# Two transformer layers with segmented memory attention on one core: the memory update in column tiles, one pool of eight PSUM banks, and a newly made order of the work

## The chip, the cores and the metric

The kernel runs on 1 core of one Trainium2 chip. The metric is device microseconds of that core. Before the change three runs took 550.18, 549.96 and 549.16 us, a median of 549.96 us.

## The reference

The input is one sequence of 2048 tokens of width 640 in bfloat16. Two equal layers follow each other, with the same weights in both:

```python
x = x + A(layernorm(x))     # attention with a memory
x = x + B(layernorm(x))     # relu(x @ w1) @ w2, inner width 1728

# A: 32 heads of 20, four segments of 512 tokens, per head and segment s:
p     = softmax(qs @ ks.T * scale + causal mask)
a_dot = p @ vs
a_mem = (phi(qs) @ M) / (phi(qs) @ z + 1e-6)   # phi(t) = t + 1 if t > 0 else exp(t)
o     = g * a_mem + (1 - g) * a_dot            # g = sigmoid(beta), one number per head
M     = M + phi(ks).T @ vs                     # memory update, used by the next segment
z     = z + sum(phi(ks))
# A returns o @ wo
```

## The kernel before

**Who sets the order.** The program is not written in the order in which it runs. Every part of the work is a generator (a stream) that hands out operations with an engine, a guessed duration and the events that they wait for. A planner, class `Sched`, runs on the host while the kernel is built. It always takes the operation that can start first by its own guesses, with priorities, a few margins and a table `SHIFT` of hand-set shifts per stream and segment, and appends it to its engine's queue. On the chip each engine then works through a fixed list. The planner's guesses are no times of the chip and are not used here.

**The work on TensorE (PE).** A segment needs K and Q (the weights stay in the array, 512 tokens stream), V, the scores, the weighted sum of V ("apply"), the memory read and the memory update, the output projection and the two products of the feed-forward part. Nearly all products run through the helper `group`, so that they carry the lines L715 (one matmul on the whole 128x128 array) or L718 (the same product as four matmuls, each on a column tile of 32 columns, which run side by side). Other lines: L1236 scores, L1330 apply, L1369 apply for two special head groups, L1116 memory read, L1173 memory update (`mem_write`), L1510 the last 64 inner columns of the feed-forward part.

**Three tile shapes.** Scores contract over 20 features, so four heads run side by side in four row tiles ("rows"). Apply and L1510 run in column tiles ("cols"). Everything else can run on the whole array ("full") or as four column tiles; `_mode` chooses: it stays in the shape that the array has, and when it comes from rows it goes to cols if a product that needs cols is near.

**Scores.** For two head groups of four heads there are five rounds of two halves, done two halves at a time: 160 visits of PE in all, each with four or eight matmuls into two pairs of PSUM banks. After each visit ScalarE (ACT) runs two exponentials over 1024 columns each (L1298), GpSimd (POOL) cuts the causal triangle (L1310), and PE applies the result to V. One visit thus feeds two exponentials, and a pair of banks comes free when its exponential is done.

**PSUM.** Eight banks of 512 float columns. Banks 0 to 3 are two pairs that belong to the scores alone (`X`, `Y`). Banks 4 to 7 (`MISC`) take every other product, each until VectorE (DVE) or ACT has copied it out; early on, banks 4 and 5 are lent to the scores as a third pair (`Z`). The memory read uses one bank of MISC at a time in all segments but one.

**The memory update.** In 6 of the 8 passes over a segment (not the last segment of a layer) `mem_write` multiplies phi(k), transposed by DMA, with V: four blocks of 128 tokens times five chunks of 128 features, as a part of three chunks and a part of two, with widths of 147 and 168. That is 20 steps per pass, 120 in all. Whole-array steps compute all head pairs of a chunk, of which only the blocks of the same head are used. In column tiles only the first block of 128 tokens does so; the other three blocks let each of the four tiles compute just the two or three heads that it holds, widths 42 or 63. Which form a step takes is left to `_mode`.

**Copies out of PSUM.** `evac` lets the planner choose ACT or DVE for each copy: L916/L917 for Q and K, L971 for V, L1340 for the applied scores, L1534/L1535 for the feed-forward part. DVE adds the output projection to x in L1452 and the feed-forward part in L1556.

Of the kernel before, what the change touches and what calls it, by code (L numbers as in the profile page):

```python
# [13 lines left out]
NSEG = 4  # L14
# [96 lines left out]

class Op:
# [4 lines left out]
    def __init__(self, alts, waits, dma=None, acq=None, urgent=False, take=(), mode="full", lag=0.0, port=False):  # L117
        self.lag = lag
        self.port = port
        self.alts = alts  # L120
        self.mode = mode
        self.cols = None
        self.cols_ns = None
        self.acq = acq
        self.waits = [t for t in waits if t is not None]
        self.dma = dma
        self.urgent = urgent
        self.take = take


class Slot:
    def __init__(self, ap=None, name=""):
# [3 lines left out]
        self.tks = []  # L136

    def release(self, *tks):
        assert not self.free, self.name
        self.tks = [t for t in tks if t is not None]  # L140
        self.free = True

# [18 lines left out]
class Spawn:  # L161
# [7 lines left out]
LONE_NS = 300.0  # L169
SWITCH_NS = 96.0  # L170
COLS_LAG = 1500.0
SOFT = 400
SOFT_DMA = 1000
SOFT_FROM = ("sc",6,4,1)
# [3 lines left out]
SHIFT = {  # L178
# [9 lines left out]
}  # L188
# [3 lines left out]
class Sched:  # L192


    def __init__(self, prog):
# [8 lines left out]
        self.soon = 0.0  # L204
        self.landed = set()
        self.done = 0
        self.seen = 0
        self.live = []

    def add(self, prio, gen):  # L210
        self.streams.append([prio, gen, None, None, False])
        self.rank[id(gen)] = 0

    def at(self, tk):
        return self.t[(id(tk[0]), tk[1])]
# [5 lines left out]
    def _fill(self, st):  # L221
        while st[2] is None and not st[4]:
            try:
                y = next(st[1]) if st[3] is None else st[1].send(st[3][0])
            except StopIteration:
                st[4] = True
                return
            st[3] = None
            st[2] = y

    def _settle(self, st):

        while True:
            self._fill(st)
            if st[4]:
                return False
            y = st[2]
            if isinstance(y, (Op, Either)):
                return True
            if isinstance(y, Spawn):  # L240
# [3 lines left out]
            elif isinstance(y, Need):  # L244
                if y.key not in self.events:
                    return False
                st[2], st[3] = None, (self.events[y.key],)
            else:
                s = self._pick(y.slots)
                if s is None:  # L250
                    return False
                s.free = False
                st[2], st[3] = None, (s,)

    def _pick(self, slots):
        return min((s for s in slots if s.free), default=None,
                   key=lambda s: max([self.at(t) for t in s.tks], default=0.0))
# [8 lines left out]
    def _alts(self, op):  # L266
        res = []
        waits = op.waits
        if op.acq is not None:
            s = self._pick(op.acq)  # L270
            if s is None:
                return res
            waits = waits + s.tks
        for k, (e, hold, fns, tail) in enumerate(op.alts):
            m = PE_MARGIN if e == "pe" else 0.0
            if op.cols_ns is not None and self._mode(op) == "cols":
                hold = op.cols_ns
            if e == "pe" and self._mode(op) != self.mode:
                hold = hold + SWITCH_NS
            start = max([self.at(t) + SEM_NS + m for t in waits], default=0.0)  # L280
            start = max(self.free[e], start)
            if e == "dve" and op.port and self.free["pool"] > start:
                hold = max(hold, self.free["pool"] - start + PORT_NS)
            res.append((start + hold, start, k, e))
        return res

    def _landing(self, op):
        start = max([self.free["pe"]] + [self.at(t) + SEM_NS + PE_MARGIN for t in op.waits])
        soft = SOFT_DMA if SOFT_FROM in self.events else 0.0
        return max([0.0] + [self.at(t) + SEM_NS + PE_MARGIN + soft - start for t in op.waits  # L290
                           if (id(t[0]), t[1]) in self.landed])

    def _late(self, op):
        late = 0.0
        if op.alts[0][0] == "pe" and SOFT_FROM in self.events:
            waits = op.waits
            if op.acq is not None:
# [1382 lines left out]
```

## Time and profile before

| | |
|---|---|
| median of 3 runs | 549.96 us (549.16 to 550.18) |
| span of the profiled execution, first to last instruction | 548.1 us |
| the profiled execution's own time | the page gives its span alone |
| PE busy | 541.5 us (99%), 9714 matmuls |
| DVE busy | 422.0 us (77%) |
| ACT busy | 411.0 us (75%), 320 exponentials of them 309.1 us |
| POOL busy | 192.6 us (35%) |
| granted TensorE clock | 1.000 |

A matmul is recorded from its start to the end of its way through the array, and the next one starts before that. So busy time says when PE had something under way, and pace must be read from starts: from the start of one group to the start of the next. Times within the span are counted from its start.

### The profile page before, as it was taken

What the parts mean: (1) busy time and instruction counts of PE and PEld (TensorE: products, weight loads), DVE (VectorE), ACT (ScalarE), POOL (GpSimd) and SP (SyncE); (2) the same over time, 40 slices, a digit from 0 to 9 for tenths busy, and PEclk for the clock granted to TensorE, in tenths of its full rate; (3) what the DMA queues carried; (4) which work ended last, traced back from release to release, by engine and by line L of the source; (5) the groups of instructions that cost most, each with busy time, mean ns of one, the idle gap of its engine ahead of it and who ended that gap; (6) DMA issues with size and microseconds to landing.
All of it is one profiled execution on the core that took longest, in us unless ns stands there. A gap on an engine that the chain in (4) does not pass through costs nothing.

```text
span 548.1 us, 21884 instructions
## 1 busy us (share of the span) xinstructions
PE 541.5 (99%) x9714; PEld 313.9 (57%) x9715; DVE 422.0 (77%) x1057; ACT 411.0 (75%) x530; POOL 192.6 (35%) x307
## 2 busy tenths in 40 slices
PE   8999999999999999999999999999999999999998
PEld 6643465466544556545555554654566646757756
DVE  5999898899998668678998985787997689717202
ACT  5999968889888777887888889779897798041140
POOL 6345532433354334433344443333234333100000
PEclk9999999999999999999999999999999999999999
DMA  9899996545567254252656934525776241531301
GB/s 302 228 188 223 222 193 135 159 97 80 70 151 163 37 88 101 60 115 76 99 173 125 140 58 122 135 20 87 112 178 93 72 68 23 106 63 16 88 2 51
DMA packets 131910, 61.96 MB, mean 113 GB/s; under 512 B 112136, under 2 KB 121864, under 8 KB 131816
## 3 DMA queue, kind: packets, MB, share of 16 engines
q1 hardware_dynamic: 131384, 60.20, 52.4%
q8 instruction: 76, 1.25, 1.0%
q10 hardware_dynamic: 432, 0.37, 0.2%
q14 instruction: 18, 0.15, 0.1%
HBM read 20.57 MB, written 12.85 MB: 61 GB/s over the span
## 4 chain that ended last, share of the span: by engine, by line
PE 92%; DVE 4%; ACT 1%; DMA 1%; POOL 0%; SPq 0%; issue 0%
PE ps L718 42%; PE ps L715 31%; PE ps L1236 9%; PE ps L1330 6%; PE ps L1116 2%; PE ps L1173 1%; PE ps L1510 1%; DVE w_r L916 1%; DMA x_sb<-in_A_x_dram 1%; DVE xn_tok L782 1%; DMA pad<-scr 1%; DVE o_sb L1424 0%; DVE stg L916 0%; PE ps L1369 0%; DVE w_r L971 0%; ACT hT L859 0%
## 5 line engine op out<-in xcount | busy, mean ns | idle before, releaser
L1298 ACT ACTIVATE PT<-ps 128x1024 bf16<-128x1024 f32 x320 | 309.1, 1025 | 54.3 <-PE ps L1236 53.2
L1310 POOL TENSOR_SCALAR_AFFINE_SELECT PT<-PT 128x512 bf16<-128x512 bf16 x256 | 165.5, 664 | 248.6 <-ACT PT L1298 248.6
L718 PE MATMUL ps<-xnT,w_r 128*32 128x512 bf16 x1360 | 81.9, 380 | 0.0
L718 PE MATMUL ps<-w_r,hT 128*32 128x320 bf16 (+1 forms) x2000 | 74.5, 296 | 0.0
L1556 DVE TENSOR_TENSOR x_sb<-x_sb,ps 128x320 bf16<-128x320 bf16 (+1 forms) x65 | 31.0, 477 | 46.9 <-PE ps L718 37.6
L1236 PE MATMUL ps<-pad 20*128 20x512 bf16 (+3 forms) x1024 | 63.4, 301 | 0.5 <-DMA pad<-scr 0.4
L718 PEld LDWEIGHTS ps<-w_r,hT 128*32 128x32 bf16 x2000 | 51.3, 97 | 14.0 <-issue 2.7
L736 DVE BATCH_NORM_STATS2 stats<-x_sb 128x6 f32<-128x320 bf16 x124 | 55.3, 475 | 3.3 <-DMA x_sb<-in_A_x_dram 2.4
L715 PE MATMUL ps<-w_r,hT 128*128 128x320 bf16 x345 | 54.7, 300 | 0.0
L718 PEld LDWEIGHTS ps<-xnT,w_r 128*32 128x32 bf16 x1360 | 34.2, 97 | 32.2 <-issue 4.5
L1535 ACT ACTIVATE hT<-ps 128x512 bf16<-128x512 f32 x52 | 31.1, 599 | 26.6 <-PE ps L718 25.4
L1534 DVE TENSOR_SCALAR hT<-ps 128x512 bf16<-128x512 f32 x52 | 35.7, 687 | 17.9 <-PE ps L718 10.2
L1236 PEld LDWEIGHTS ps<-pad 20*128 20x128 bf16 x1024 | 17.9, 92 | 49.6 <-issue 24.0
L715 PE MATMUL ps<-xnT,w_r 128*128 128x512 bf16 x180 | 43.9, 380 | 0.0
L752 POOL TENSOR_TENSOR rstd<-lnU,mhalf 128x2 f32<-128x2 f32 (+2 forms) x26 | 20.6, 793 | 61.7 <-DVE lnU L748 61.0
L1452 DVE TENSOR_TENSOR x_sb<-x_sb,ps 128x320 bf16<-128x320 bf16 x64 | 29.6, 469 | 15.9 <-PE ps L718 15.1
L715 PEld LDWEIGHTS ps<-w_r,hT 128*128 128x128 bf16 x345 | 31.5, 98 | 16.3 <-issue 4.9
L1330 PE MATMUL ps<-PT,v_aug 128*21 128x128 bf16 (+3 forms) x896 | 40.2, 299 | 0.0
L916 DVE CAST stg<-ps 128x512 bf16<-128x512 f32 (+1 forms) x48 | 31.1, 648 | 9.8 <-PE ps L715 6.1
L782 DVE TENSOR_SCALAR xn_tok<-x_sb,mv,rstd 128x640 bf16<-128x640 bf16 x60 | 30.9, 543 | 4.9 <-POOL rstd L752 4.7
L1424 DVE TENSOR_TENSOR o_sb<-otk,rden 128x320 bf16<-128x320 bf16 x62 | 32.6, 550 | 0.4
L1087 DVE TENSOR_TENSOR phs<-phs,rtmp 128x512 bf16<-128x512 bf16 x60 | 30.2, 504 | 3.2 <-ACT phs L1086 2.4
(121 smaller groups left out, 742.2 us busy)
## 6 DMA issues: line engine op xcount, KB each, us to landing
pad<-scr SPq DMA_DIRECT2D x124, 80.0 KB
scr<-stg SPq DMA_DIRECT2D x34, 256.0 KB, 2.9
out_dram<-x_sb SPq DMA_DIRECT2D x15, 160.0 KB, 2.1
w_r<-in_B_w_dram SPq DMA_DIRECT2D x10, 216.0 KB, 3.2
w_r<-in_B_w_dram SPq DMA_DIRECT2D x13, 160.0 KB, 2.8
x_sb<-in_A_x_dram SPq DMA_DIRECT2D x10, 160.0 KB, 5.1
scr<-w_r SPq DMA_DIRECT2D x5, 256.0 KB, 3.4
wk_r<-in_A_wk_dram SPq DMA_DIRECT2D x1, 800.0 KB, 7.3
```

The source lines that it names most:

```text
L715: return e.matmul(view(dst.ap, b), a, b, start=(k == 0), stop=(k == last))
L718: return e.matmul(view(dst.ap[rows], b), part, b, start=(k == 0), stop=(k == last))
L736: tk = yield dve(320, 1, lambda e, c2=c2: e.bn_stats(stats6[:, t, c2, :], x_sb[:, t, c2 * 320:(c2 + 1) * 320]), xt)
L782: nm = lambda e, bx, t, k: e.tensor_scalar(bx.ap[:, k * D:k * D + D], x_sb[:, t + k, :], mv[:, t + k, 0:1], rstd[:, t + k:t + k + 1], ALU. ...
L916: te = yield evac(N, 1, lambda e: e.tensor_copy(sg.ap[:, t0:t0 + N], bk.ap[:, 0:N]), lambda e: e.activation(sg.ap[:, t0:t0 + N], bk.ap[:, ...
L1236: fns.append([(lambda e, z=z, j=j, hh=hh, N=N, o=o, sl=sl, q=hh % 2: e.matmul(slot.ap[:, q, o:o + N], sl.ap[32 * hh:32 * hh + DH, z, 0, 12 ...
L1298: tx = yield act(1024, lambda e, dst=dst, src=src: e.activation(dst, src, ACT.Exp, scale=SCALE), sc + pw)
L1310: tm = yield pool(600.0, lambda e, reg=reg: e.affine_select(out=reg, in_=reg, pattern=[[0, 4], [1, 128]], compare_op=ALU.is_ge, fill=0.0, ...
L1330: fns.append((lambda e, OD, j=j, hh=hh: e.matmul(OD.ap[32 * hh:32 * hh + DH + 1, 128 * j:L], VAUG[vx(a, s)][:, j, 4 * g + hh, :], pt.ap[:, ...
L1424: to = yield dve(320, 1, lambda e, z=z, dst=dst: e.tensor_tensor(dst, av[:, z, :, :, 0:DH], rd.ap[:, z].to_broadcast([128, NJ, 4, DH]), AL ...
L1534: th = yield evac(512, 1, lambda e: e.tensor_scalar(hT[:, dc, :], bk.ap[:, :], 0.0, None, ALU.max), lambda e: e.activation(hT[:, dc, :], b ...
L1535: lambda e: e.activation(hT[:, dc, :], bk.ap[:, :], ACT.Relu), [tk] + HT.tks)
```

## The change

Four things change in the code; none changes what is computed.

1. **Memory update.** `_mode` now sends a product that has a price of its own for column tiles (`cols_ns`) to cols whenever the array comes from rows. `mem_write` gives such a price to its first block too, and a lag `WRITE_LAG` of 1500 ns that puts it off while the array is in the full shape. So it comes behind scores, in column tiles.
2. **PSUM.** `X`, `Y`, `Z` and `MISC` give way to one pool `Banks`. Scores may take any two of the four pairs (0,1), (2,3), (4,5), (6,7) that are free. Other products may take any free bank, up to a number that the planner's way of the moment sets (2, 3 or 4 of them, or all while the next scores have no input). One of the ways keeps the split of before. The memory read now takes any bank, but one at a time (`ONE`).
3. **Order.** The planner's clock is cut into stretches of 10 us. For each stretch a number from the table `SEEDS` picks one of ten ways (the bank limit, and how far score visits are kept apart) and a pattern of small shifts per stream (`shake`). `SHIFT` keeps its numbers.
4. **Planner.** Its loop is rewritten (`settle`, `look`), a score visit waits for the previous one plus the way's distance, and the "lone" half visit goes, which was never offered.

```diff
+class Banks:
+    def pick(self, S):
+        low, lim = (6 if S.lent else 4, 4) if S.way[2] else (0, len(self.slots) if self.open else S.way[1])
+        if self.held("misc") >= lim:
+            return None
+        free = [(S.slot_at(s), k, s) for k, s in enumerate(self.slots) if s.free and k >= low]
+        if not free:
+            return None
+        now = [x for x in free if x[0] + SEM_NS + PE_MARGIN <= S.free["pe"]]
+        if now and not low:
+            return max(now, key=lambda x: (self.near(x[1]), x[0], -x[1]))[2]
+        return min(free)[2]
+    def pairs(self, S):
+        ks = (0, 2, 4, 6) if not S.way[2] else (0, 2, 4) if S.lent else (0, 2)
+        got = [(max(S.slot_at(s) for s in self.slots[k:k + 2]), k) for k in ks
+               if self.slots[k].free and self.slots[k + 1].free]
+        if len(got) < 2:
+            return None
+        return [self.twos[k // 2] for _, k in sorted(got)[:2]]
...
+WRITE_LAG = 1500.0
-SOFT_FROM = ("sc",6,4,1)
+SOFT_FROM = ("vis", 34)
...
+WIN = 10000.0
+SEEDS = [381981813, 8, 9, 51464074, 8, 0, 933685753, 8, 9, 9, 8, 3, 8, 5, 552090255, 1036812015, 127496082,
...
+WAY = [(0.0, 4, True), (0.0, 2, False), (1300.0, 2, False), (1600.0, 2, False), (0.0, 3, False), (1300.0, 3, False),
+       (1600.0, 3, False), (0.0, 4, False), (1300.0, 4, True), (1600.0, 4, True)]
...
         if self.mode != "rows":
             return self.mode
+        if op.cols_ns is not None:
+            return "cols"
         return "cols" if self.soon < self.free["pe"] + 2500 else "full"
...
-                key = (round(start + late + SHIFT.get((n, self.rank[id(st[1])]), 0)), 0.5 if op.urgent else prio, self.rank[id(st[1])], n)
+                key = (round(start + late + SHIFT.get((n, rank), 0) + shake(self.seed, n)), 0.5 if op.urgent else prio, rank, n)
...
-        X = Slot(ps[:, 0:2, :], "SX")
-        Y = Slot(ps[:, 2:4, :], "SY")
-        Z = Slot(ps[:, 4:6, :], "SZ")
-        MISC = [Slot(ps[:, 4 + k, :], "misc%d" % k) for k in range(4)]
-        LENT = MISC[0:2]
-        SC = [X, Y]
+        BK = [Slot(ps[:, k, :], "bank%d" % k) for k in range(8)]
+        MISC = Banks(BK, [Slot(ps[:, 2 * k:2 * k + 2, :], "two%d" % k) for k in range(4)])
+        MISC.open = True
+        ONE = Slot(None, "one")
...
-                    bk, tk = yield either(pe(60.0 * len(lst), fns, phi + bdt, acq=MISC if (a, s) == (0, 1) else MISC[:1]), cols)
+                    one = (a, s) != (0, 1)
+                    if one:
+                        yield Acq([ONE])
+                    bk, tk = yield either(pe(60.0 * len(lst), fns, phi + bdt, acq=MISC), cols)
...
-                            bk, lastd = yield either(pe(66.0 * len(cs), fns, pht + vt, acq=MISC), cols)
+                            bk, lastd = yield either(pe(66.0 * len(cs), fns, pht + vt, acq=MISC, lag=WRITE_LAG), cols, 64.0 * len(cs))
```

What this makes of the order is seen best at two places. Names: `pad` holds the heads for the scores, `PT` the exponentials, `v_aug` V with a column of ones, `phk` the transposed phi(k), `hT` the inner values of the feed-forward part, `w_r` any weight. Lines of the changed kernel stand some 110 higher: L1349 scores, L1444 apply, L1288 memory update, L823/L826 the helper, L1411 exponentials.

**PE, the second segment of the first layer, first part of its memory update.** Before, PE's queue reads:

```order
L1236 MATMUL ps<-pad 128x512 x4
L715 MATMUL ps<-w_r,hT 128x320
L715 MATMUL ps<-w_r,hR 128x320
L1173 MATMUL ps<-v_aug,phk 128x147 x2
L1173 MATMUL ps<-v_aug,phk 128x168
L1173 MATMUL ps<-v_aug,phk 128x147 x2
L1173 MATMUL ps<-v_aug,phk 128x168
L1173 MATMUL ps<-v_aug,phk 128x147 x2
L1173 MATMUL ps<-v_aug,phk 128x168
L1173 MATMUL ps<-v_aug,phk 128x147 x2
```

In the changed kernel the same update stands in PE's queue like this:

```order
L1349 MATMUL ps<-pad 128x384 x4
L1349 MATMUL ps<-pad 128x128 x4
L826 MATMUL ps<-w_r,hT 32x320 x24
L826 MATMUL ps<-w_r,hR 32x320 x4
L1444 MATMUL ps<-PT,v_aug 21x512 x4
L1444 MATMUL ps<-PT,v_aug 21x384 x4
L1444 MATMUL ps<-PT,v_aug 21x256 x4
L1444 MATMUL ps<-PT,v_aug 21x128 x4
L1349 MATMUL ps<-pad 128x256 x8
L1288 MATMUL ps<-v_aug,phk 32x147 x8
L1288 MATMUL ps<-v_aug,phk 32x168 x4
L1288 MATMUL ps<-v_aug,phk 32x42
```

The twelve whole-array steps have become quarters of column tiles right behind a score visit, twelve wide ones and then narrow ones. Two score visits also stand closer together than before: nothing but one round of column tiles is between them.

**ACT, the first segment of the first layer, from the exponentials of the fifth score visit on.** Before, ACT's queue reads:

```order
L1298 ACTIVATE PT<-ps 128x2x512 x2
L1086 ACTIVATE phs<-w_r 128x512
L917 ACTIVATE w_r<-ps 128x512
L1298 ACTIVATE PT<-ps 128x2x512 x4
L1298 ACTIVATE PT<-ps 128x2x2x256 x2
L1298 ACTIVATE PT<-ps 128x2x512 x8
L1298 ACTIVATE PT<-ps 128x2x2x256 x2
L1298 ACTIVATE PT<-ps 128x2x512 x8
L1298 ACTIVATE PT<-ps 128x2x2x256 x2
L1298 ACTIVATE PT<-ps 128x2x512 x6
L1086 ACTIVATE phs<-w_r 128x512
L917 ACTIVATE stg<-ps 128x512
```

In the changed kernel ACT's queue reads, from the same exponentials on:

```order
L1411 ACTIVATE PT<-ps 128x2x512 x2
L1196 ACTIVATE phs<-w_r 128x512
L1411 ACTIVATE PT<-ps 128x2x512 x4
L1454 ACTIVATE otu<-ps 128x512
L1026 ACTIVATE w_r<-ps 128x512
L1196 ACTIVATE phs<-w_r 128x512
L1411 ACTIVATE PT<-ps 128x2x2x256 x2
L1196 ACTIVATE phs<-w_r 128x512
L1411 ACTIVATE PT<-ps 128x2x512 x8
L1411 ACTIVATE PT<-ps 128x2x2x256 x2
L1411 ACTIVATE PT<-ps 128x2x512 x8
L1411 ACTIVATE PT<-ps 128x2x2x256 x2
```

Before, all exponentials of these visits stand back to back with no other work among them; now four other instructions (a copy of applied scores, a copy of K or Q, two for phi) stand between the early ones.

More of the change, by code (lines that the diff above doesn't have):

```diff
@@ L141, in release, with __init__, held, near @@
         self.free = True
+class Banks:
+    def __init__(self, slots, twos):
+        self.slots = slots
+        self.twos = twos
+        self.open = False
+        for k, two in enumerate(twos):
+            two.banks = slots[2 * k:2 * k + 2]
+    def held(self, user):
+        return sum(1 for s in self.slots if not s.free and s.user == user)
+    def pick(self, S):
[9 more added lines that the diff above has]
+        return min(free)[2]
+    def near(self, k):
+        s = self.slots[k ^ 1]
+        return not s.free and s.user == "misc"
+    def pairs(self, S):
[5 more added lines that the diff above has]
+        return [self.twos[k // 2] for _, k in sorted(got)[:2]]
 class Acq:
@@ L349, in run @@
                 for end, start, k, e in alts:
[L350 to L352 removed]
+                    for p2, st2, (_, s2, _, e2) in hold:
+                        if p2 < prio and st2 is not st and e2 == e and s2 + HOLD_TOL[e] < end:
+                            break
+                    else:
                         ok.append((end, start, k))
```

328 lines of the change are left out of this document (191 added, 137 removed), and 17 rows, old and new, of the table SHIFT.

## The prediction

> **What bounds the kernel now.** I read the page's busy table first, then windows of the span, then the waits of PE.
>
> ```profile
> span 548.1 us, 21884 instructions
> PE 541.5 (99%) x9714; PEld 313.9 (57%) x9715; DVE 422.0 (77%) x1057; ACT 411.0 (75%) x530; POOL 192.6 (35%) x307
> ...
> PE 92%; DVE 4%; ACT 1%; DMA 1%; POOL 0%; SPq 0%; issue 0%
> ```
>
> PE is the bound: 541.5 of 548.1 us busy, and 92% of the chain that ended last is PE's own. But a matmul counts as busy until it has left the array, so short waits hide in these numbers. The windows show where PE is not fed (the columns are PE, PEld, DVE, ACT and POOL busy, then the granted clock, the DMA share and rate).
>
> ```profile
> 20.00:30.00 10.00, 9.81 (x94) 6.47 (x93) 10.00 (x28) 9.42 (x15) 3.88 (x6) 1.00 0.79 154
> 30.00:40.00 10.00, 9.49 (x98) 3.60 (x97) 9.54 (x25) 9.41 (x11) 5.15 (x8) 1.00 0.95 202
> 40.00:50.00 10.00, 9.10 (x142) 4.27 (x140) 9.13 (x19) 9.75 (x12) 5.55 (x9) 1.00 1.01 201
> 50.00:60.00 10.00, 9.81 (x125) 3.79 (x125) 8.82 (x18) 10.00 (x12) 5.22 (x9) 1.00 0.97 205
> 60.00:100.00 40.00, 40.00 (x546) 23.57 (x548) 36.11 (x99) 32.81 (x46) 14.69 (x22) 1.00 0.82 192
> 100.00:200.00 100.00, 100.00 (x1524) 54.28 (x1516) 84.95 (x203) 84.75 (x107) 40.00 (x60) 1.00 0.52 103
> ...
> 450.00:500.00 50.00, 50.00 (x1214) 32.76 (x1206) 30.63 (x87) 22.43 (x32) 8.04 (x12) 1.00 0.27 54
> 500.00:540.00 40.00, 40.00 (x1044) 28.48 (x1035) 11.65 (x30) 8.53 (x15) 1.39 (x2) 1.00 0.19 44
> ```
>
> So there are two regimes. From 60 us on PE is never idle and nothing but PE work counts. Between 20 and 60 us PE is idle for 0.19 + 0.51 + 0.90 + 0.19 = 1.79 us, and ACT is busy for 9.4 to 10.0 of every 10 us: there the exponentials set the pace. ACT's timeline says so more sharply (start, length, and how many instructions run on without a break).
>
> ```profile
> 33.64 7.56 ACT L1298 ACTIVATE PT<-ps 128x1024 bf16<-128x1024 f32 x8
> 41.36 22.42 ACT L1298 ACTIVATE PT<-ps 128x1024 bf16<-128x1024 f32 x24 [0.17 <-PE ps L1236]
> 63.67 0.63 ACT L1086 ACTIVATE phs<-w_r 128x512 bf16<-128x512 bf16 x1
> 64.19 0.60 ACT L917 ACTIVATE stg<-ps 128x512 bf16<-128x512 f32 x1
> ...
> 67.44 1.94 ACT L1298 ACTIVATE PT<-ps 128x1024 bf16<-128x1024 f32 x2 [0.30 <-PE ps L1236]
> ```
>
> From 33.64 to 63.67 ACT runs 32 exponentials with a pause of 0.17 us: 0.94 us each, 1.88 us for a score visit. In that stretch a microsecond saved on PE is a microsecond waited.
>
> **The change, part by part.** *Memory update.* The forms of the groups count its whole-array steps before.
>
> ```profile
> L1173 PE MATMUL ps<-v_aug,phk 128*128 128x147 bf16 x32 | 3.4, 228 | 0.0
> L1173 PE MATMUL ps<-v_aug,phk 128*128 128x168 bf16 x10 | 2.1, 233 | 0.0
> L1173 PE MATMUL ps<-w_r,phk 128*128 128x147 bf16 x8 | 0.9, 227 | 0.0
> L1173 PE MATMUL ps<-w_r,phk 128*128 128x168 bf16 x4 | 0.8, 234 | 0.0
> ```
>
> That is 32 + 10 + 8 + 4 = 54 of the 120 steps; the other 66 were in column tiles already. The new order has all 480 quarters in column tiles and no whole-array step, so the change does what it says here. Of the 54 steps 14 belong to first blocks, which stay wide, and 40 become narrow. The mean of 228 ns is the way through the array; the pace is in the starts.
>
> ```profile
> 124.72 0.97 PE L1173 MATMUL ps<-v_aug,phk 128*128 128x147 bf16 x12
> 125.53 1.25 PE L715 MATMUL ps<-w_r,hT 128*128 128x320 bf16 x8
> ```
> ```profile
> 436.54 0.46 PE L1173 MATMUL ps<-v_aug,phk 128*32 128x147 bf16 x32
> 436.85 0.73 PE L1510 MATMUL ps<-xnT,w_r 128*32 128x256 bf16 x20
> 437.51 0.40 PE L1236 MATMUL ps<-pad 20*128 20x512 bf16 x4
> 437.83 2.33 PE L715 MATMUL ps<-xnT,w_r 128*128 128x512 bf16 x10
> ```
> ```profile
> 480.55 14.21 PE L718 MATMUL ps<-xnT,w_r 128*32 128x512 bf16 x260
> ```
>
> Twelve whole-array steps take 125.53 - 124.72 = 0.81 us, 67.5 ns each. In column tiles a second part (32 quarters: two wide steps and six narrow ones, in one row of mixed forms) takes 436.85 - 436.54 = 0.31 us. The 260 quarters at 480.55 are 65 steps of 512 columns in about 14.0 us, the last one's way through the array left off: 0.216 us a step, 0.42 ns a column. A wide step of 147 columns is then 0.062 us, and six narrow ones share 0.31 - 0.12 = 0.19 us, 0.031 us each; by their columns alone (63) it would be 0.026. So 54 x 67.5 = 3.65 us go, and 14 x 0.062 + 40 x 0.031 = 2.11 us come: **1.5 us less**, 1.7 at most. It counts in full wherever PE is the bound.
>
> The Trainium skill speaks against this form: "TensorEngine Tiling (Array Packing)", Performance Considerations, under Instruction Overhead, gives every matmul some 60 cycles however few columns it has, and advises against tiling a dimension that is already small. At its 60 cycles (25 ns at 2.4 GHz), paid one after another, my estimate is 54 x 4 x 25 ns = 5.4 us against 3.65, a loss of 1.75 us. The quoted 32 quarters in 0.31 us, 10 ns each, say that four tiles pay it side by side.
>
> *Changes of shape.* Counted over the whole order there are 321 before and 322 after. The rows above price one: 437.83 - 437.51 less one step of 0.216 is 0.10 us, and 437.51 - 436.85 less five steps of 256 columns (0.54) is 0.12. One more costs 0.1 us. Products of `group` and the memory read that move between full and cols keep their columns, which cost the same either way. So PE's work falls by **1.4 to 1.6 us**; I take 1.5.
>
> *The new order, first 70 us.* Up to the fourth score visit the order is as before. PE's work up to the 23rd visit (its exponentials are at 67.44 above), counted at 0.42 ns a column and the prices of a change, grows from 58.0 to 59.6 us, so behind it 1.6 + 1.5 = 3.1 us less remain. But that visit waits on ACT. From the exponentials of the sixth visit to those of the 23rd ACT has 34 exponentials in both orders. Before, three other instructions stand among them (0.63, 0.60 and one more at 0.63); now six (two copies at 0.60, four for phi at 0.63). That is 3.7 - 1.9 = 1.8 us more. In exchange one copy no longer stands ahead of the sixth visit's exponentials.
>
> ```profile
> 32.31 0.63 ACT L1086 ACTIVATE phs<-w_r 128x512 bf16<-128x512 bf16 x1 [0.43 <-DVE w_r L916]
> 33.09 0.60 ACT L917 ACTIVATE w_r<-ps 128x512 bf16<-128x512 f32 x1 [0.16 <-PE ps L718]
> ```
>
> So they can start 0.6 to 1.1 us before 33.64, bounded by the heads that must land first. The 23rd visit then comes 0.7 to 1.2 us later with 3.1 us less behind it: the end moves by -1.9 to -2.4 us, the 1.5 us of the memory update included. I take **-2.0**, nearer to the end at which ACT has some pauses, as before. If ACT's extra work is not absorbed at all, it is 3.1 - 1.8 = -1.3.
>
> *The pool.* 49 of the 160 visits now use banks other than the old four; before it was 11, all early. These banks may have been emptied by a copy on DVE rather than by an exponential, and the planner gives scores no extra margin against that. Before the change no row shows a score waiting for a bank that DVE empties late, so I bound it: below by nothing; above by one copy in the way, for each of the 49.
>
> ```profile
> L916 DVE CAST stg<-ps 128x512 bf16<-128x512 f32 (+1 forms) x48 | 31.1, 648 | 9.8 <-PE ps L715 6.1 <-PE ps L718 3.0
> ```
>
> That end is 49 x 0.65 = 32 us. I take nothing: from 60 us on the old pool's four banks, emptied by the same copies at 85% of DVE, never left PE idle (100.00 of 100.00 above). The cover is other PE work put between copy and visit; where it is gone, a visit waits, and every product queued behind it on PE waits too.
>
> *The end.* The last visit has 73 us of PE work behind it instead of 80, so the last segment's attention has less cover. Between the last apply and the output projection that needs it stand 17.6 us (25.6 before). The trace has this road: copy, DMA transpose, division, transposes.
>
> ```profile
> 468.85 0.60 ACT L1340 ACTIVATE otu<-ps 128x512 bf16<-128x512 f32 x1 [1.85 <-PE ps L1330]
> 469.47 2.01 SPq L758 DMA_TRANSPOSE otk<-otu  x1
> ...
> 473.23 0.35 DVE L1416 RECIPROCAL rden<-otk 128x32 f32<-128x32 bf16 x1
> ...
> 473.84 0.89 DVE L1424 TENSOR_TENSOR o_sb<-otk,rden 128x320 bf16<-128x320 bf16 x2
> ...
> 481.69 3.20 SPq L758 DMA_TRANSPOSE oT<-o_sb  x2
> ```
>
> From 468.85 to 474.73 are 5.9 us, one sum on DVE 0.5, the two transposes with their landing some 5: under 12 us. It stays hidden; if it did not, each microsecond over 17.6 would be paid.
>
> **The sum.** -1.5 (PE's work), -0.5 (first 70 us), 0 (pool), 0 (end): a span of 548.1 - 2.0 = 546.1 us. The runs' median lies 549.96 - 548.1 = 1.9 us above the profiled span; with the same distance the time is **548.0 us**.
>
> **The rivals.** *New waits at the shared banks (slower).* For it: ACT and DVE are at 85% from 100 to 200 us, 49 visits depend on other banks, and visits come as close as 1.8 to 2.0 us of PE work, two exponentials' time. Against it: PE's old record with DVE-emptied banks. The point is a mean wait: at 2.0 / 49 = 0.04 us per visit the gain is gone, at 0.065 us it is slower by over 0.2%. At 0.1 us, a sixth of one copy, it is 4.9 us: 549.96 - 2.0 + 4.9 = 552.9 us. The Trainium skill's page "TensorEngine Tiling (Array Packing)", Performance Considerations, PSUM Bottleneck, says that tiling quickens TensorE but not the copies out of PSUM, which may become the bottleneck. The 9.4 to 10.0 of 10 us on ACT above agree with it for the first 60 us only.
>
> *The saving turns into waiting (no change).* Where ACT is the bound, PE's saving is waited away: 12 of the 54 steps lie before 60 us, 0.3 us. With ACT's extra 1.8 us not absorbed at all, and a few short waits for copies (0.1 us, six of them), it is -1.3 + 0.3 + 0.6 = -0.4: 549.6 us.
>
> *Narrow tiles pay a floor one after another (slower).* If each of the 216 added quarters held PE like a whole step, 216 x 67.5 ns = 14.6 us against 3.65: 560.9 us. The 0.31 us row excludes nearly all of it.
>
> **How the numbers follow.** Forecast 0.60 (546.5 to 548.8), no change 0.19, new waits 0.19, floor 0.02. The low end takes 1.7 for the update, the 0.9 that the first 70 us can give, 0.3 for the copies' luck and 0.5 for the spread of the runs (549.16 to 550.18): 549.96 - 3.4 = 546.5. The high end goes into the waits, to 0.075 us per visit: 548.0 + 3.7 = 551.7; the forecast alone would end at 548.8. A measurement of this kernel can tell about 0.2%, 1.1 us, from no change: faster 0.60, same 0.19, slower 0.21.
>
> **What would show it.** L1173's successor has only forms with 32 columns, its parts take 0.31 and about 0.46 us. PE idle between 20 and 60 us stays between 1 and 2.5 us, the exponentials of the 23rd visit start near 68.3 us, and PE is busy for all of 60 to 540 us. I am wrong if the waits of PE list scores behind DVE after 60 us, if the output projection waits for a transpose near the end, or if the 23rd visit comes after 69.5 us.

## The result and the profile after

The changed kernel takes 551.79 us (551.70 to 552.43, 5 runs) against 549.92 us (549.16 to 550.18, 5 runs) before: a ratio of 1.0038 [1.0026, 1.0050], 1.9 us slower. The forecast was 2.0 us faster. The profiled execution of the changed kernel took 551.71 us with a span of 549.9 us (548.1 before).

Two lines of the page answer to the first fence of the prediction: the busy table and the engines' shares of the chain that ended last.

```profile
PE 541.0 (98%) x9943; PEld 310.7 (57%) x9943; DVE 420.4 (76%) x1064; ACT 408.8 (74%) x523; POOL 194.5 (35%) x307
...
PE 84%; DVE 11%; DMA 1%; ACT 1%; issue 1%; POOL 1%; DVEq 0%
```

PE is as busy as before, but its share of the chain fell from 92% to 84% and that of DVE rose from 4% to 11%: the end now leads back through other engines. The windows of the changed kernel say where (columns as in the prediction):

```profile
20.00:30.00 10.00, 9.89 (x97) 6.24 (x99) 10.00 (x29) 9.37 (x14) 3.88 (x6) 1.00 0.79 160
30.00:40.00 10.00, 10.00 (x213) 4.90 (x210) 9.75 (x26) 9.67 (x13) 5.11 (x6) 1.00 0.91 175
40.00:50.00 10.00, 9.29 (x118) 3.77 (x115) 9.74 (x21) 9.31 (x11) 5.02 (x8) 1.00 0.94 208
50.00:60.00 10.00, 9.90 (x114) 3.79 (x114) 9.20 (x21) 9.95 (x12) 5.46 (x9) 1.00 0.85 233
60.00:80.00 20.00, 20.00 (x220) 11.63 (x219) 17.46 (x49) 16.55 (x22) 8.41 (x14) 1.00 0.89 214
80.00:90.00 10.00, 8.57 (x208) 5.76 (x209) 7.52 (x22) 8.62 (x13) 4.79 (x8) 1.00 1.07 181
...
100.00:200.00 100.00, 99.62 (x1765) 52.96 (x1758) 79.37 (x195) 88.51 (x112) 40.53 (x61) 1.00 0.56 105
...
300.00:400.00 100.00, 99.48 (x2132) 55.05 (x2124) 82.97 (x208) 81.25 (x101) 35.56 (x55) 1.00 0.53 106
400.00:450.00 50.00, 49.79 (x960) 28.22 (x953) 40.22 (x109) 45.42 (x56) 22.06 (x34) 1.00 0.38 83
```

Between 20 and 60 us PE is idle for 0.92 us, half of the 1.79 before. Behind 60 us, where it was never idle, it is now idle for 1.43 us in one stretch, and for 0.2 to 0.5 us in three others. The waits of PE from 60 to 540 us name them (engine, tile and line, what it waited for, then total, times and longest):

```profile
PE ps L1624 <- issue: 1.0, 1, 1.0
PE ps L1349 <- ACT PT L1411: 0.4, 1, 0.4
PE ps L826 <- DMA xnT<-xn_tok: 0.3, 1, 0.3
PE ps L1444 <- DVE hT L1648: 0.3, 1, 0.3
PE ps L823 <- DVE hR L1630: 0.2, 1, 0.2
PE ps L1349 <- DVE M_sb L1306: 0.2, 1, 0.2
PE ps L826 <- DVE stg L1025: 0.2, 1, 0.2
```

The same list of the kernel before is empty. Idle time shows only what is left of a wait when the last matmul has left the array, so I also take, for each product, its start less PE's work ahead of it (counted as in the prediction). This lag grows when PE waits, seen or unseen:

| PE's work done, us | 50 | 75 | 80 | 100 | 200 | 300 | 400 | 533 |
|---|---|---|---|---|---|---|---|---|
| lag before, us | 7.87 | 9.18 | 9.19 | 9.20 | 9.24 | 9.24 | 9.24 | 10.61 |
| lag after, us | 6.94 | 8.26 | 9.83 | 10.13 | 11.00 | 11.62 | 12.11 | 13.56 |

Behind 400 us both rows rise by 1.4 us, though PE waits nowhere there before: the counted prices are not exact, so only the difference of the two rows is read. Against before the new order is 0.92 us ahead at 75, loses 1.56 at one place just behind it, and another 2.3 in small steps up to the end: +2.9 us of lag, with 1.5 us less work. The last store, issued at 546.17 us before and at 547.56 after, agrees (+1.4); it then took 1.9 us to land instead of 1.5, which makes the 1.8 us between the spans.

What happens near 88 us is seen in PE's timeline, first before, then after (output projection `wo_r`, then the first steps of the feed-forward part, which need its result):

```profile
70.40 1.79 PE L715 MATMUL ps<-wo_r,oT 128*128 128x320 bf16 x12
...
75.20 1.67 PE L715 MATMUL ps<-wo_r,oT 128*128 128x320 bf16 x11
...
88.00 0.38 PE L715 MATMUL ps<-xnT,w_r 128*128 128x512 bf16 x1
...
88.64 0.73 PE L1510 MATMUL ps<-xnT,w_r 128*32 128x256 bf16 x20
```
```profile
72.07 1.66 PE L823 MATMUL ps<-wo_r,oT 128*128 128x320 bf16 x11
...
76.73 1.80 PE L823 MATMUL ps<-wo_r,oT 128*128 128x320 bf16 x12
...
86.92 0.40 PE L1349 MATMUL ps<-pad 20*128 20x256 bf16 x8 [0.43 <-ACT PT L1411]
88.32 0.73 PE L1624 MATMUL ps<-xnT,w_r 128*32 128x256 bf16 x20 [1.00 <-issue]
```

The projection comes 1.67 us later than before. From its last step (78.24 us) its result goes through additions, layernorm and DMA transposes; the last transpose lands at 88.23 us by the trace's events, 0.09 us ahead of L1624. So "issue" in the row hides a DMA. Before, that chain ended at 86.42 us, and PE reached the first step of the feed-forward part at 88.00, 1.6 us later.

Why the projection is late stands in ACT's timeline after:

```profile
36.55 0.60 ACT L1454 ACTIVATE otu<-ps 128x512 bf16<-128x512 f32 x1
37.03 0.62 ACT L1026 ACTIVATE w_r<-ps 128x512 bf16<-128x512 f32 x1
37.51 0.65 ACT L1196 ACTIVATE phs<-w_r 128x512 bf16<-128x512 bf16 x1
38.03 1.96 ACT L1411 ACTIVATE PT<-ps 128x1024 bf16<-128x1024 f32 x2
39.84 0.67 ACT L1196 ACTIVATE phs<-w_r 128x512 bf16<-128x512 bf16 x1
...
64.46 5.67 ACT L1411 ACTIVATE PT<-ps 128x1024 bf16<-128x1024 f32 x6
```

The four instructions stand among the exponentials; those of the 23rd visit start at 64.46 + 4 x 0.945 = 68.2 us (67.44 before). PE meanwhile ran V, for which it need not wait, and then had too little left to put between the projection and the feed-forward part.

### The profile page after: what moved, and what is told of

Same layout as the page of the kernel before. It is cut to its first block, busy times and chain, and to the rows that moved or that the text cites. A ratio compares the mean times of both kernels' runs of the same rounds, so it can differ in the third digit from the quotient of the medians.

```text
span 549.9 us, 22357 instructions
## 1 busy us (share of the span) xinstructions
PE 541.0 (98%) x9943; PEld 310.7 (57%) x9943; DVE 420.4 (76%) x1064; ACT 408.8 (74%) x523; POOL 194.5 (35%) x307
## 4 chain that ended last, share of the span: by engine, by line
PE 84%; DVE 11%; DMA 1%; ACT 1%; issue 1%; POOL 1%; DVEq 0%
PE ps L826 40%; PE ps L823 27%; PE ps L1349 8%; PE ps L1444 6%; DVE xn_tok L890 2%; PE ps L1226 1%; DVE stats L844 1%; DVE hT L1648 1%; DMA xnT<-xn_tok 1%; DVE o_sb L1538 1%; PE ps L1624 1%; DVE phs L1197 1%; ACT PT L1411 1%; DVE w_r L1025 1%; PE ps L1288 1%
## 5 line engine op out<-in xcount | busy, mean ns | idle before, releaser
L1411 ACT ACTIVATE PT<-ps 128x1024 bf16<-128x1024 f32 x320 | 308.4, 1026 | 56.2 <-PE ps L1349 54.8
L1424 POOL TENSOR_SCALAR_AFFINE_SELECT PT<-PT 128x512 bf16<-128x512 bf16 x256 | 167.6, 673 | 257.1 <-ACT PT L1411 256.9
L826 PE MATMUL ps<-xnT,w_r 128*32 128x512 bf16 x1492 | 89.0, 379 | 0.1
L826 PE MATMUL ps<-w_r,hT 128*32 128x320 bf16 (+1 forms) x1996 | 74.6, 296 | 0.0
L1349 PE MATMUL ps<-pad 20*128 20x512 bf16 (+3 forms) x1024 | 63.4, 301 | 0.7 <-ACT PT L1411 0.4
L826 PEld LDWEIGHTS ps<-w_r,hT 128*32 128x32 bf16 x1996 | 51.2, 97 | 13.9 <-issue 1.7
L826 PEld LDWEIGHTS ps<-xnT,w_r 128*32 128x32 bf16 x1492 | 37.6, 97 | 35.3 <-issue 3.9
L823 PE MATMUL ps<-w_r,hT 128*128 128x320 bf16 x346 | 54.4, 300 | 0.0
L1649 ACT ACTIVATE hT<-ps 128x512 bf16<-128x512 f32 x50 | 29.9, 598 | 24.0 <-PE ps L826 21.6
L1349 PEld LDWEIGHTS ps<-pad 20*128 20x128 bf16 x1024 | 17.8, 92 | 52.1 <-issue 25.6
L823 PEld LDWEIGHTS ps<-w_r,hT 128*128 128x128 bf16 x346 | 31.8, 98 | 16.2 <-issue 4.8
L1444 PE MATMUL ps<-PT,v_aug 128*21 128x128 bf16 (+3 forms) x896 | 40.3, 300 | 0.3 <-DVE hT L1648 0.3
L1454 DVE CAST otu<-ps 128x512 bf16<-128x512 f32 x46 | 31.5, 684 | 8.3 <-PE ps L1444 7.9
L823 PE MATMUL ps<-xnT,w_r 128*128 128x512 bf16 x147 | 35.9, 380 | 0.0
L1025 DVE CAST stg<-ps 128x512 bf16<-128x512 f32 (+1 forms) x44 | 28.1, 647 | 7.3 <-PE ps L823 5.2
L890 DVE TENSOR_SCALAR xn_tok<-x_sb,mv,rstd 128x640 bf16<-128x640 bf16 x60 | 29.0, 513 | 4.0 <-POOL rstd L860 3.9
L1197 DVE TENSOR_TENSOR phs<-phs,rtmp 128x512 bf16<-128x512 bf16 x60 | 28.6, 478 | 4.5 <-ACT phs L1196 3.3
```

The costliest lines, as they stand in the source:

```text
L823: return e.matmul(view(dst.ap, b), a, b, start=(k == 0), stop=(k == last))
L826: return e.matmul(view(dst.ap[rows], b), part, b, start=(k == 0), stop=(k == last))
L890: nm = lambda e, bx, t, k: e.tensor_scalar(bx.ap[:, k * D:k * D + D], x_sb[:, t + k, :], mv[:, t + k, 0:1], rstd[:, t + k:t + k + 1], ALU. ...
L1025: te = yield evac(N, 1, lambda e: e.tensor_copy(sg.ap[:, t0:t0 + N], bk.ap[:, 0:N]), lambda e: e.activation(sg.ap[:, t0:t0 + N], bk.ap[:, ...
L1197: tp = yield dve(512, 2, lambda e, rt=rt, dst=dst: e.tensor_tensor(dst, dst, rt.ap, ALU.min), [te, tr])
L1349: fns.append([(lambda e, z=z, j=j, hh=hh, N=N, o=o, sl=sl, q=hh % 2: e.matmul(slot.ap[:, q, o:o + N], sl.ap[32 * hh:32 * hh + DH, z, 0, 12 ...
```

## The experiments

Times are medians, ratios are against the kernel before in the same session. The first theories were: the 88 us wait comes from ACT's extra work (A), the small waits from the shared banks (B).

**e1_write_only.** Before's order; the five whole-array blocks go behind the next score visit.

```diff
         if self.mode != "rows":
             return self.mode
+        if op.cols_ns is not None:
+            return "cols"
...
-memory update, 12 whole-array steps
 score visit
+memory update, 48 quarters
```

> The kernel before in its old order and with its old banks, with one thing of the change alone: the blocks of the memory update that ran on the whole array are put behind the next score visit, where they run as column tiles. All else stands where it stood. Theory: the form itself saves what I counted, 1.5 to 1.7 us of PE's work, and in the old order PE is never idle behind 60 us, so the time falls by the same: 548.2 to 548.5 us. Rival: the column tiles bring waits of their own (later memory, later banks), so that at most 0.4 us are left: 549.5 us or more.

550.87 us (550.48 to 552.57), ratio 1.0023 [1.0015, 1.0032]. With 1.7 us less work on PE the kernel is slower: the rival. PE's timeline at the block that stood at 124.72 us:

```profile
123.79 0.40 PE L1495 MATMUL ps<-pad 20*128 20x512 bf16 x4
...
126.49 0.40 PE L1495 MATMUL ps<-pad 20*128 20x384 bf16 x8 [0.70 <-ACT PT L1557]
126.81 0.66 PE L1432 MATMUL ps<-v_aug,phk 128*32 128x147 bf16 x48
...
129.72 0.40 PE L1495 MATMUL ps<-pad 20*128 20x256 bf16 x8
```

The three visits stood at 124.11, 126.84 and 129.59 us: 5.48 us from first to third. Now it is 5.93. The 0.81 us of the block had been the cover between two visits; the second one cannot come sooner than its exponentials allow, and the 0.46 us of quarters stretch the next distance. A saving of 0.35 us became a loss of 0.45.

**e5_swap.** The same with the distance kept (and the first segment's block left as it was).

```diff
-memory update, 12 whole-array steps
+five steps of the feed-forward part
 score visit
-five steps of the feed-forward part
+memory update, 48 quarters
```

> The kernel before in its old order and with its old banks; four of the five blocks of the memory update go into column tiles (12 whole-array steps of the first segment stay), three of them behind the next score visit, one behind an apply. Other than in e1_write_only, steps of the feed-forward part or of the output projection (three, five and two) go ahead of that visit in the block's place, so that no two visits come closer than about 2.5 us. PE's work counts 1.3 us less than before. Theory: e1 lost its saving because the block had been the cover between two visits that stand 2.73 us apart, 0.37 us behind their exponentials; with the distance kept the saving stays: 548.5 to 548.9 us. Rival: the column tiles themselves, or what comes behind them, wait: 549.5 us or more.

550.59 us (549.72 to 554.19), ratio 1.0016 [1.0003, 1.0028]: the rival again. No score waits for its exponentials behind 60 us any more; others wait. PE and then DVE in its trace:

```profile
139.88 0.34 PE L1375 MATMUL ps<-BD,phs 128*128 128x147 bf16 x3 [0.63 <-DVE om_sb L1390]
```
```profile
139.33 0.49 DVE L1390 TENSOR_TENSOR om_sb<-ps,rmem 128x320 bf16<-128x320 f32 x1
```

In the old order this copy (at 138.90) ended 0.11 us ahead of the memory read at 139.50. PE came 0.4 us earlier, DVE 0.4 us later; why DVE came later is not shown.

**e9_less_update and e15_less_again.** The old order with nothing moved; part of the update is left out (see the expectation).

```diff
+                        fns = [] if i in (1, 2) else fns
                         if i == 0:
```

> The kernel before in its old order, with nothing moved, but with part of the computation left out: in each whole-array block of the memory update the second and third of the four blocks of 128 tokens are not multiplied (27 steps of 67.5 ns less), so its memory is not the reference's. PE's work counts 1.7 us less. Theory D (no reserve): the chains of the other engines stand only 0.05 to 0.4 us behind PE, so most of what PE saves is waited away at the next score visit or copy: 549.4 to 550.2 us. Rival: PE is the bound, and e1 and e5 lost their saving only because work was moved: 548.1 to 548.5 us.

550.18 us (549.50 to 551.37, 11 runs), ratio 1.0004 [0.9996, 1.0013]: 1.7 us less work, and the time did not fall. Its profiled execution was its quickest, so a second one was traced:

> e9_less_update once more, unchanged (part of the memory update left out), since its profiled execution was its fastest (549.5 us, where its median is 550.18). Theory D: a usual execution loses the saving of 1.7 us in waits that its trace names, ahead of the output projection near 71 us and at visits or copies behind it. Rival: the lost time stands outside the span or in the first 20 us, where the inputs land.

550.96 us. PE's waits from 60 to 540 us:

```profile
PE ps L972 <- DMA oT<-o_sb: 0.7, 1, 0.7
PE ps L972 <- issue: 0.5, 1, 0.5
PE ps L1494 <- ACT PT L1556: 0.2, 1, 0.2
```

The first is the output projection at 71.11 us, waiting for its transpose, the second the feed-forward part at 88.95 us, waiting for its own: the two ends of the first segment's chain. At 75 us of work the lag is 1.1 us above before's, at 80 it is 1.7, and from there to 380 it stays within 0.1. The first 20 us, where the inputs land, are as before (5.56 us of lag, 5.59 before).

A lag that stays level means that PE's time falls by all the work that is left out. The same two score visits show it, in before, e9 and e15:

```profile
99.30 0.40 PE L1236 MATMUL ps<-pad 20*128 20x384 bf16 x8
458.16 0.40 PE L1236 MATMUL ps<-pad 20*128 20x256 bf16 x8
```
```profile
99.60 0.40 PE L1494 MATMUL ps<-pad 20*128 20x384 bf16 x8
457.52 0.40 PE L1494 MATMUL ps<-pad 20*128 20x256 bf16 x8
```
```profile
100.24 0.40 PE L1494 MATMUL ps<-pad 20*128 20x384 bf16 x8
458.46 0.40 PE L1494 MATMUL ps<-pad 20*128 20x256 bf16 x8
```

Up to the first of them 0.8 us of work is left out, and yet both traces reach it later than before, by 0.30 and 0.94 us: between 38 and 47 us, where the exponentials set the pace, the traces lose 0.6 us against the work, and at the late transposes e9 another 0.4 us (71 us), e15 0.9 (71 us) and 0.6 (89 us). Between the two visits 1.0 us is left out; e9 gains 0.94 there, e15 0.64 (one visit waits 0.23 us for exponentials). So less work does pay behind 89 us, and the loss stands ahead of it. Each piece left out behind 89 us is 0.4 us or less, about what a score visit has in reserve (0.37 us at the block of e1, which moved 0.81 away); that this is the reason is read from the numbers, not tested. Whether leaving work out made the transposes late, or their landings vary by as much (last section), is not shown.

**e10_before_more_work.** The other direction.

```diff
-                    fns = [(mm, last == 0)]
+                    fns = [(lambda e, dst, m=mm: m(e, dst, one=True), False)] * again + [(mm, last == 0)]
```

> The kernel before with eight more matmuls of 320 columns (a repeat of the first product of a V group, 1.07 us of PE's work) behind the first segment's output projection; order, banks and result stay. Theory D and PE as the bound say the same here: nothing hides more work on PE, 550.9 to 551.1 us. Against both: a hidden wait of PE takes it up, 550.3 us or less. Beside e9 it tells whether PE's work counts in both directions.

550.97 us, ratio 1.0022 [1.0013, 1.0030]: 1.2 us for 1.07 us of work, in full. More work costs what it takes. Less work did not shorten the time in e1, e5 and e9; in the first two it was waited away at visits and a copy that had little reserve, in e9 it was lost ahead of 89 us.

**e13_after_again and e14_before_again.** Both kernels once more, for a second trace each.

> The changed kernel once more, unchanged, for a second execution's trace. If its waits belong to the order, they stand at the same places: the feed-forward part near 88 us again 1.0 us idle ahead of its first product, and three or more of the small ones (94.8, 113, 310, 369 and 416 us) again, PE's idle time behind 60 us 2.3 to 3.3 us by the windows. If they are luck of single landings, other places wait, or the sum is below 1.5 us.

> The kernel before once more, unchanged. If waiting nowhere behind 60 us belongs to its order, the windows show PE busy for all of 60 to 540 us again. If it was luck, 0.5 us or more of idle time stands there.

551.72 and 550.07 us. The list of the changed kernel:

```profile
PE ps L1624 <- issue: 0.8, 1, 0.8
PE ps L1349 <- ACT PT L1411: 0.4, 1, 0.4
PE ps L826 <- DMA xnT<-xn_tok: 0.3, 1, 0.3
...
```

All seven recur, the four others with 0.2 us each (idle time behind 60 us by the windows 2.57 us, 2.60 in the first trace), and the list of before is empty again: both belong to the orders, not to luck.

**e3_old_split_late.** From 90 us on the old split.

```diff
-SEEDS = [381981813, 8, 9, 51464074, 8, 0, 933685753, 8, 9, 9, 8, 3, 8, 5, 552090255, 1036812015, 127496082,
+SEEDS = [381981813, 8, 9, 51464074, 8, 0, 933685753, 8, 9, 0, 0, 0, 0, 0, 0, 0, 0,
...
```

> The changed kernel, planned anew with the old split of the banks and no small shifts from the tenth stretch (90 us) on; the order up to 90 us stays. Theory B: PE's small waits behind 90 us (2.3 us more than in the kernel before) come from the shared banks and the tight order made with them; with the old split they go, and the gap at 88 us stays: 549.4 to 549.9 us. Rival: they come from something that the split does not decide (the update behind scores, the planner's other rules): 551.3 us or more.

553.12 us (551.82 to 554.06), ratio 1.0061 [1.0048, 1.0074]. The rival: with the old split the waits do not go, so theory B falls as it was put. By the windows of its profiled execution, its quickest (551.82 us), PE is idle for 1.72 us behind 90 us (1.17 in the changed kernel), at other places. That does not clear the pool altogether. The run also makes a new order behind 90 us, and of the changed kernel's seven waits two are at banks that only the pool allows: the score visit L1349 at 113.18 us waits for bank 7, which DVE's `M_sb` empties, and L826 at 156.15 us for bank 3, which `stg` empties, 0.2 us each.

**e4_work_in_gap.** The changed kernel with 1.07 us of work repeated at 85 us (the edit of e10).

> The changed kernel with eight more matmuls of 320 columns (a repeat of the first product of a V group, about 1.07 us of PE's work), put between the first segment's output projection and the feed-forward part, at about 85 us; order, banks and result stay. Theory A: PE waits there 1.4 us for the chain, which has left PE by then; so the added work falls into the wait and costs 0 to 0.3 us: 551.8 to 552.1 us. Rival: PE is the bound there as it is later, and the work costs its full length: 552.8 to 553.0 us.

552.59 us (551.70 to 556.22), ratio 1.0057 [1.0037, 1.0078]: the time alone decides nothing. PE's timeline does:

```profile
84.86 2.75 PE L823 MATMUL ps<-wv_r,hT 128*128 128x320 bf16 x19
87.54 0.40 PE L1349 MATMUL ps<-pad 20*128 20x256 bf16 x8
88.08 0.73 PE L1624 MATMUL ps<-xnT,w_r 128*32 128x256 bf16 x20
```

Both waits are gone, and L1624 starts 0.24 us earlier than in the changed kernel (88.32; e13: 88.03) with 1.07 us more work ahead. From the last step of the projection to it are 9.8 us; in the changed kernel 10.1 (e13: 9.8), with 8.6 us of work there. The wait near 88 us is for the chain. This profiled execution, the slowest of the six, then lost 2.4 us at another place (last section).

**e2, e6, e7, e11, e12: attempts to bring the chain forward.** Edits in the changed kernel's order: phi behind the 20th visit's exponentials (e2; spread over three visits in e11); five steps of V behind the output projection (e6; with DVE's copy of them moved too in e12); two copies on DVE (e7).

```diff
+e2, e11: ACT: phi behind the exponentials of visit 20 (e11: of 20, 21, 22)
-e6, e12: PE: V x7, output projection x11
+e6, e12: PE: V x2, output projection x15 ... V x26
-e7: ACT: otu<-ps, w_r<-ps
+e7: DVE: otu<-ps, w_r<-ps
```

> The changed kernel with the early phi work of ACT and DVE (first layer, first segment) put behind the exponentials of the 20th score visit; PE's work and banks stay. Theory A: the four extra ACT instructions among the first exponentials made the first segment's chain (exponentials, apply, division, output projection, layernorm, transposes) late, so that PE stands at the feed-forward part near 88 us. Two of them, for phi, go: the chain comes about 1.2 us earlier, the wait of 1.0 us near 88 us is gone or nearly so, and the time falls by about 1.0 to 1.2 us from 551.8: 550.6 to 550.8 us. Rival: the wait near 88 us has another cause, or is given back by later waits: 551.5 us or more.

> The changed kernel with five steps of V (0.67 us) moved from ahead of the first segment's output projection to behind it; the score visits keep their places, the other steps move up. Theory A: the wait near 88 us is for the chain output projection, layernorm, transpose; the chain starts 0.6 us earlier, so the feed-forward part starts near 87.7 us instead of 88.32, and the time falls by about 0.6 us: 551.0 to 551.3 us. Rival: the wait is for something else, the start stays near 88.3 and the time at 551.8 us.

> The changed kernel with two of the four extra instructions among the first exponentials (a copy of applied scores and a copy of K, 0.60 us each) on DVE instead of ACT; the order stays. Theory A: ACT sets the pace of the first segment's chain, so its exponentials come 0.6 to 1.2 us earlier, and so does the transpose that PE waits for near 88 us: the wait shrinks by 0.5 to 1.0 us, 550.8 to 551.3 us. Rival: DVE is busy for nine tenths there and the two copies delay the chain as much as ACT did: 551.6 us or more.

> e2 once more without its bunching: the changed kernel with the two early instructions for phi behind the exponentials of the 20th and 21st visit and one more behind the 22nd, so that no three stand together. Theory A: the first segment's exponentials, and so its output projection (first step at 72.07 us, in the old order at 70.40), come 0.6 to 1.2 us earlier, the wait near 88 us shrinks by as much: 550.7 to 551.3 us. Rival: what ACT gains is lost at another engine of that chain, 551.6 us or more.

> e6 once more, with DVE's copy of the moved V group behind the last addition of the output projection; in e6 it stood ahead of the additions and held them up by 1.3 us. Theory A': from the last step of the output projection to the first of the feed-forward part the chain takes 9.8 to 10.1 us, whatever PE does between (after, e4, e7), and the new order has 8.6 us of PE work there. The projection ends 0.6 us earlier with 0.67 us more work behind it: the feed-forward part starts near 87.7 us, and the time falls by 0.5 to 0.7 us: 551.1 to 551.3 us. Rival: the start stays near 88.3 us and the time at 551.8 us or more.

562.67, 556.11, 554.86, 562.75 and 554.28 us, ratios 1.0230 [1.0217, 1.0243], 1.0108 [1.0095, 1.0121], 1.0089 [1.0076, 1.0102], 1.0238 [1.0224, 1.0252] and 1.0078 [1.0066, 1.0091]. All missed. In e2 and e6 the trace names a wait that the move itself made. In e2 ACT, in order, waits for phi's buffer with the exponentials behind it:

```profile
69.25 0.63 ACT L1453 ACTIVATE phs<-w_r 128x512 bf16<-128x512 bf16 x1 [4.56 <-DMA phk<-phs]
```

In e6 a copy of V on DVE waited for its product with the last additions behind it:

```profile
79.08 0.49 DVE L1338 CAST v_aug<-ps 128x320 bf16<-128x320 f32 x1 [0.68 <-PE ps L1081]
```

In the other three only the times are read. In e7 the projection came at 73.03 us, later than in the changed kernel, and L1882 waited 0.92 us (there 1.00); in e11 it came at 79.95 us; in e12 at 71.94 (72.07 in the changed kernel), yet the feed-forward part at 88.54. So theory A is not shown by experiment. That ACT's four instructions made the chain late is read from the timelines; what relieves it stays open.

**e8_no_shift.** Before, planned anew without the hand-set shifts.

```diff
-SHIFT = {
-    (2, 0): 50, (5, 0): -500, (7, 0): -5450, (7, 6): -2050, (8, 3): -100, (8, 6): -100, (8, 7): 1350,
...
+SHIFT = {}
```

> The kernel before, planned anew without the table of hand-set shifts; banks, rules and the update as before. By its order PE's work counts 0.8 us more than before (72 whole-array steps, 323 changes of shape). Theory C: an order that the planner makes anew meets late copies and transposes that its guesses do not know, and waits behind 60 us as the changed kernel does (2 to 4 us in all); the old order waits nowhere because the table was set for it: 552.5 to 555 us. Rival: the planner's own margins are enough, and only PE's work counts: 550.5 to 551 us.

562.88 us (562.38 to 564.93), ratio 1.0239 [1.0222, 1.0256]: theory C's direction, at three times its size. Old code, old banks, old rules, and scores alone wait 5.4 us for exponentials in its trace; part of the loss is the clock, granted at 0.50 for 10.2 us from 165.5 us on (last section). Waiting nowhere behind 60 us is a property of the order that the table makes, and not of the old code.

No experiment pointed to a version that beats both kernels.

## Why the prediction was wrong, point by point

- **What bounds the kernel.** "From 60 us on PE is never idle and nothing but PE work counts" is the step that failed. It was read from the old order and carried over to the new one, so that waits behind 60 us stood in the sum at nothing. For the old order the first half is right, twice traced. In the new order PE is idle for 2.60 us behind 60 us, and its lag against before grows by 3.9 us from 75 us of work to the end (-0.92 to +2.95). The second half holds for added work (e10: 1.07 us cost 1.2). For work taken away it holds only where what PE awaits next has a reserve: behind 89 us in e9 (0.94 of 1.0 us gained), but neither at the block of e1 (0.70 us of waiting) nor at the memory read of e5 (0.63).
- **Memory update.** Right as work: all forms have 32 columns, the parts take 0.46 (82.14 to 82.60 us) and 0.30 us, PE's work falls by 1.5 us. "It counts in full wherever PE is the bound" did not hold as time where the update went behind a score visit (e1, e5).
- **New order, first 70 us.** The 23rd visit came at 68.2 us (forecast 68.3), PE's idle time was 0.92 us (1 to 2.5). "3.1 us less" work behind that visit was put down as a gain without asking what else the late visit delays: the chain to the feed-forward part came 1.8 us later and took 1.56 us back at one place. Before, PE reached the feed-forward part only 1.6 us behind the landing (86.42 to 88.00), so a delay of that size could not stay hidden.
- **Pool.** Forecast nothing; two seen waits of 0.2 us, one of them a score visit behind DVE after 60 us, which the prediction had named as a sign of being wrong. The rival's sign was right; its mechanism is seen in these two waits alone. The other late waits (0.2 to 0.3 us each, at a transpose, an operand and a copy out of a bank that took the same work before) are at no bank that the pool opened. What brings how much of the 2.3 us, the pool, the update behind scores or the new plan, stays open.
- **Changes of shape, the end, and the distance of span and time.** Right: no wait behind 417 us, 1.8 us between span and time.
- **The rival nearest in mechanism** was "the saving turns into waiting", but I let it act ahead of 60 us only, and so priced it at no change.
- **The sum, as measured on PE:** -1.5 (work), -0.9 (start), +1.6 (near 88 us), +2.3 (behind), that is about +1.4, and 0.4 for the last store.

## What to carry to other kernels

Before a saving on a full engine is counted, look for the reserve of what that engine waits for next: the margin between each wait's end and the start that it allows. Where those margins are a few tenths of a microsecond, as here (119 of the 140 score visits behind 60 us started less than 0.45 us behind the exponential that empties their banks, one memory read 0.11 us behind its copy), a larger saving turns into waiting, and an order made anew has to earn its margins again. Ask of every piece of work that moves what it had been covering.

## What was not expected of the hardware

A long wait costs more than itself. In e4's profiled execution a division on DVE waited 2.5 us for a DMA transpose, the next copy stood behind it, and a score visit behind that; the windows show PE and, in the column ahead of the last two, the granted clock:

```profile
174.00:176.00 2.00, 0.00 (x0) 0.00 (x0) 2.00 (x4) 0.00 (x0) 1.03 (x2) 1.00 0.79 285
176.00:177.00 1.00, 0.77 (x6) 0.34 (x7) 0.82 (x4) 0.34 (x1) 0.00 (x0) 1.00 0.35 123
177.00:178.00 1.00, 1.00 (x5) 0.45 (x4) 0.68 (x1) 1.00 (x2) 0.00 (x0) 0.77 0.56 158
178.00:179.00 1.00, 1.00 (x3) 0.30 (x2) 0.56 (x1) 1.00 (x2) 0.33 (x1) 0.50 0.63 182
```

After 2.4 us of idleness the clock was granted at 0.50 until 181 us, and the five matmuls of 512 columns at 178.19 us took 0.43 us each instead of 0.216 (1.1 us), the six ahead of them 1.63 instead of 1.30 us (0.3): some 1.4 us on top of the 2.4. In e11 PE was idle for 2.29 and 2.34 us (from 65.29 and 72.20 us), and each time the clock was granted at 0.50 by its end; so it was in e8 behind two waits close together (1.24 and 1.00 us, from 162.68 us on). The single waits of 1.0 us near 88 us (changed kernel) and of 1.17 us at 33 us (e8) did not lower it. The Trainium skill, "TensorE: Matmul & The Clock Gate", Part 1, describes this halving, but after an idle window of about 3.4 us; here 2.3 to 2.4 us were enough.

The other surprise is how much a transpose's landing varies. In e9 and e15, the same program, the last transposes ahead of the feed-forward part landed at 87.26 and 88.86 us, where the first of them was issued at 80.39 and 80.77. An order with tenths of a microsecond in reserve inherits that spread: e9 ran from 549.50 to 551.37 us, e4 from 551.70 to 556.22.
